# Fourier mixing and soft mixture of experts: batch 0's first transform with the tokens stationary, reordered on chip, and batch 1 in fp32r throughout

## The chip, the cores and the metric

One core of a Trainium2 chip. A core has TensorE (PE, matmuls; PEld is its weight load), VectorE (DVE), ScalarE (ACT), GpSimd (POOL) and SyncE (SP, which here only issues DMAs). The metric is the time of one execution of the whole kernel in microseconds (us), measured on the device; lower is better.

## The reference

```python
x = attn_in                                  # 8 batches, 2496 tokens, 256 wide, float32
X = np.fft.rfft(x, axis=1)                   # over the tokens
Yr = Xr @ w_r - Xi @ w_i + b_r
Yi = Xr @ w_i + Xi @ w_r + b_i
Y  = sign(Y) * max(|Y| - 0.01, 0)            # real and imaginary part apart
y  = np.fft.irfft(Y, n=2496, axis=1)         # 19968 tokens of 256 from here
logits = y @ phi                             # 32 slots, 4 for each of 8 experts
d = softmax of logits over the tokens;  c = softmax of logits over the slots
slot_in = d.T @ y
slot_out[e] = max(slot_in[e] @ w1[e], 0) @ w2[e]
out = c @ slot_out
```

## The kernel before

2496 is 39 times 64, so the transform over the tokens is done in two steps: a **first transform** of length 39 and a **second** of length 64. A batch's tokens lie in 117 partitions (3 groups of 39) by 22 columns g of 256 numbers. By the symmetry of real input 20 of the 39 frequencies are enough, each with a cosine and a sine: 3 x 40 = 120 rows.

*First transform* (`a_unit`, one unit for two of the 22 columns). The constant matrix f1a (117 x 120) is stationary and the tokens move, 512 columns at a time. The result `pa` (120 rows) is copied from PSUM to `ast` by ACT, written to DRAM (`adr`; for the first 48 rows of batch 0 a tensor `ad0`, over ACT's own DMA queue) and read back by `load_ap` as `ap`, with a frequency's 64 columns in the partitions: the transposition between the two transforms goes through DRAM. In batches 2 to 7 a unit is done in fp32r: the tokens and the matrix are split into a rounded high part and the rest (`xh`, `xl`, `f1h`, `f1l`), and three fp32r matmuls are added up. In batch 0 (11 units) and in the first four units of batch 1 it is a plain fp32 matmul (`direct`), which the machine runs as two passes.

*The main loop* has 40 steps s: 8 batches by 5 groups of 4 frequencies. In a step:
- `f2`: two second transforms `px` (c = 0, 1: the left and right half of the 256 numbers), four fp32 matmuls each with a slice of `ap` stationary. ACT copies them to `xth` and `xsm`, DVE makes the rest `xtl`, a sum `xsm`, and its split `xsh`, `xsl` (POOL makes `xsl` after step 0).
- `lin_k`, `lin_y`: the linear layer in fp32r, `pk` of 12 and `py` of 24 matmuls, with the split weights `w_r`, `nws`, `wd` of the tensor `wri`. DVE and POOL add the bias and threshold (`ut`, `rt`).
- `tp_p`, `tp_t`: the logits `pq`, and transposes `pt` of `rt`, which ACT copies to `T`.

Around these run, with time stamps of their own, the first transforms of later batches, the softmax stages of earlier ones (`c_stages`), and after TB the expert weights, the experts and the output.

The order of all this is set by hand. A generator yields a due time from PLAN, `run_until` resumes the one that is due, and every operation is kept in program order on its engine. So an engine's queue is a fixed list, and an instruction that waits holds up what is behind it on that engine. In the opening the order of SP's queue was `PLAN["seq"]`: loads of constants and x, the loads of `ap` 0, 1 and 2, the four writes of the rest of batch 0, and two held writes of batch 1. PSUM tiles come from tags: `pf` (px, pa), `pl` (pk, py) and `pt` (pq, pt) with two banks each; a new tile of a tag waits until the old one in its bank has been read.

The profile's lines: L180 is the wrapper through which DVE, ACT and POOL operations are recorded, L237 is SP's DMA, L240 ACT's DMA, L243 a matmul, L532 a transpose.

Of the kernel before, what the change touches and what calls it, by code (L numbers as in the profile page):

```python
# [50 lines left out]
def _constants():  # L51
# [92 lines left out]
    "ws": [-29, -28.9, -28.8, 2],  # L144
# [3 lines left out]
    "kw": [[-40, 9]],  # L148
    "ap1": 1.85,
# [34 lines left out]
def fourier_soft_moe_kernel(ctx: ExitStack, tc: tile.TileContext, t: dict, out: bass.AP):  # L184
# [29 lines left out]
    cnt = {}  # L214
# [7 lines left out]
    def L_(k, s, i):  # L222
# [66 lines left out]
    while len(x0) < G // GP:  # L289
        load_x0()  # L290
# [35 lines left out]
    def a_unit(b, g, u):  # L326
        first = b == 0
        i_ = g // GP
        abounds = abounds_.get(b, abounds_[2])
        tu = u if first else PLAN["a1"][i_] if b == 1 else 20 * (b - 1) - LEAD + (2 * i_ + PLAN["au"][0] if i_ < 9 else PLAN["au"][i_ - 8])  # L330
        gs = next(a for a in abounds if a[0] <= g < a[1])
        direct = first or (b == 1 and i_ < PLAN["nd"])
# [6 lines left out]
        xs = x0[i_] if first else xrs[(b, g - g % xc)][:P1, g % xc : g % xc + GP, :]
        if not direct:  # L340
            xh = wtile([P1, GP, D], F32R, "xh", f"xh{b}_{g}")
            xl = wtile([P1, GP, D], F32R, "xl", f"xl{b}_{g}")
            if b == 1:
                split(xh, xl, xs, {"A": A, "V": V}[PLAN["h1"][i_]], {"P": P, "V": V}[PLAN["l1"][i_]])
            else:
                split(xh, xl, xs, E_("ah"), E_("al"))
        yield tu
        if g == gs[0]:
            if (b, g) in PLAN["ast4"]:
                asts[(b, g)] = wtile([QA, 4, D], F32, PLAN["ast4"][(b, g)], f"ast{b}_{g}")  # L350
            else:
                asts[(b, g)] = wtile([QA, 6, D], F32, "ast", f"ast{b}_{g}")
        ast = asts[(b, gs[0])]
        po = psum(("pf", "pl", "pt")[i_ % 3] if first else "pf", f"pa{b}_{g}")
        if direct:
            mm(out=po, lhsT=f1a, rhs=xs, start=True, stop=True)
        else:
            mm(out=po, lhsT=f1h, rhs=xh, start=True, stop=False)
            mm(out=po, lhsT=f1h, rhs=xl, start=False, stop=False)
            mm(out=po, lhsT=f1l, rhs=xh, start=False, stop=True)  # L360
        yield tu + PLAN['ao']
        copy(
            (A, V)[PLAN["e1"][i_]] if b == 1 else A,
            ast[:, g - gs[0] : g - gs[0] + GP, :].rearrange("p g d -> p (g d)"),
            po,
        )
        if g + GP == gs[1]:
            if b == 1 and direct:
                held[gs[0]] = (ad[b], ast, *gs)
                return  # L370
            yield tu + 1.0
            if first:
                a_write(ad0, ast, *gs, 0, R * 4 * KG, q=aq)
                rest.append((ad[b], ast, *gs, R * 4 * KG, QA))
            else:
                a_write(ad[b], ast, *gs)

    ad0 = dr.tile([R * 4 * KG, G, D], F32, tag="ad0", name="ad0", bufs=1)
    rest, held = [], {}

    def a_write(adr, ast, g0, g1, r0=0, r1=QA, q=sp):
        q(out=adr[r0:r1, g0:g1], in_=ast[r0:r1, : g1 - g0, :])
# [9 lines left out]
    def f2(s, c, t0):  # L392
# [21 lines left out]
        sl = wtile([128, KG, 64], F32R, "xsl", f"xsl{b}_{grp}_{c}")  # L414
        A.copy(out=xh, in_=pv)
# [7 lines left out]
        (L_("sl", s, c) if s else V).tensor_tensor(out=sl, in0=sm, in1=sh.bitcast(F32), op=ALU.subtract)  # L423
        xts[(s, c)] = (xh, xl, sh, sl)
# [20 lines left out]
    def lin_k(s):  # L445
# [10 lines left out]
    def lin_y(s, e):  # L456
# [318 lines left out]

    def wsplit2(nm, src, eh, el):
# [42 lines left out]
    for tok in PLAN["seq"]:  # L819
        one(tok)  # L820
# [442 lines left out]
```

## Time and profile before

| | |
|---|---|
| timed runs | 567.23, 565.03, 566.69 us; median 566.69 |
| profiled execution, span from first to last instruction | 561.5 us; it has no other time of its own, and the median lies 5.2 us above the span |
| PE busy | 521.4 us (93%), mean granted clock 0.989 |
| DVE, ACT, POOL busy | 422.0, 298.1, 281.1 us |
| DMA | 121.44 MB, mean 216 GB/s |

The span in 40 slices of 14 us, busy share in tenths (9 is 90% or more), and the granted clock of PE:

```profile
PE   8669999999999999999999999999899979899794
PEclk9999999999999999999999999999999998999899
```

PE is below 9 tenths in the first three slices (42 us) and here and there in the last ten; between them it is full. The chain of waits for the opening, the windows of 5 us and the timeline of each engine are the views to read here; their lines stand where they are used.

### The profile page before, as it was taken

How to read it: one execution, taken by the hardware profiler on the slowest of the kernel's cores; microseconds unless marked ns; L12 is line 12 of the kernel's file. 1: busy time of each engine (PE TensorE's matmuls, PEld its weight loads, DVE VectorE, ACT ScalarE, POOL GpSimd, SP SyncE). 2: the span in 40 equal slices, each digit the busy share in tenths (PEclk: the TensorE clock that was granted, in tenths of full speed). 3: DMA queues.
4: the chain of work that ended last, by engine and by line, in shares of the span. 5: the costliest groups of instructions: out<-in, count | busy, mean ns of one | idle time of the engine just before them, and what ended most of it. 6: DMA issues, size and time to landing. Idle time of an engine off the chain costs nothing.

```text
span 561.5 us, 11780 instructions
## 1 busy us (share of the span) xinstructions
PE 521.4 (93%) x4354; PEld 442.2 (79%) x4354; DVE 422.0 (75%) x837; ACT 298.1 (53%) x650; POOL 281.1 (50%) x258
## 2 busy tenths in 40 slices
PE   8669999999999999999999999999899979899794
PEld 4458999989898889889988898987687867367573
DVE  0347897799979897989789978986795764248783
ACT  4435555666566656665665666653433333147572
POOL 0037777766766576658655866684554402000100
PEclk9999999999999999999999999999999998999899
DMA  8788464756476637664757474766634378979898
GB/s 301 249 294 292 151 207 152 210 179 170 163 216 207 189 118 208 207 180 167 204 171 199 155 201 167 222 230 178 186 131 126 113 183 276 392 240 368 325 374 351
DMA packets 93684, 121.44 MB, mean 216 GB/s; under 512 B 46786, under 2 KB 68736, under 8 KB 93628
## 3 DMA queue, kind: packets, MB, share of 16 engines
q1 hardware_dynamic: 93372, 119.63, 65.4%
q10 hardware_dynamic: 256, 1.08, 0.5%
q8 instruction: 34, 0.56, 0.4%
q14 instruction: 22, 0.18, 0.1%
HBM read 69.87 MB, written 50.82 MB: 215 GB/s over the span
## 4 chain that ended last, share of the span: by engine, by line
PE 70%; DVE 13%; DMA 10%; ACT 3%; issue 2%; SPq 1%; ACTq 0%; DVEq 0%
PE py L243 16%; PE px L243 11%; PE pq L243 9%; PE pa L243 8%; PE pk L243 7%; PE pt L532 4%; PE pr L243 3%; DMA eb<-ed 2%; PE pc L1067 2%; DMA ad<-ast 2%; PE pe L243 2%; DMA ap<-adr 2%; DVE mx L180 1%; DVE clpL L180 1%; DVE xtl L180 1%
## 5 line engine op out<-in xcount | busy, mean ns | idle before, releaser
L180 POOL TENSOR_TENSOR rt<-ut,rt 128x512 f32<-128x512 f32 x79 | 111.7, 1414 | 24.4 <-DVE rt L180 18.4
L180 POOL TENSOR_TENSOR xsl<-xsm,xsh 128x256 fp32r<-128x256 f32 x77 | 59.3, 770 | 102.4 <-DVE xsh L180 71.0
L180 POOL TENSOR_TENSOR xl<-xr,xh 117x512 fp32r<-117x512 f32 x73 | 98.5, 1350 | 22.6 <-ACT xh L180 14.7
L243 PE MATMUL px<-smov,ap 128*128 128x128 f32 x640 | 85.6, 277 | 8.0 <-DMA ap<-adr 4.5
L243 PEld LDWEIGHTS px<-smov,ap 128*128 128x128 f32 x640 | 80.3, 193 | 13.7 <-issue 8.1
L180 ACT CAST xth<-px 128x512 fp32r<-128x512 f32 x80 | 46.8, 585 | 73.0 <-PE py L243 37.6
L180 ACT COPY ast<-pa 128x512 f32<-128x512 f32 x86 | 50.3, 587 | 64.5 <-PE pa L243 61.6
L180 DVE SCALAR_TENSOR_TENSOR ut<-py,pk,k 128x256 f32<-128x256 f32 x160 | 69.5, 475 | 15.0 <-PE py L243 13.1
L180 DVE TENSOR_TENSOR xtl<-px,xth 128x512 fp32r<-128x512 f32 x80 | 54.6, 682 | 26.8 <-ACT xsm L180 22.0
L243 PE MATMUL py<-xth,nwsh 128*128 128x256 f32 x160 | 53.5, 334 | 0.0
L180 DVE TENSOR_SCALAR rt<-ut 128x512 f32<-128x512 f32 x69 | 52.2, 756 | 0.5
L243 PE MATMUL pk<-xsh,w_rh 128*128 128x256 f32 x160 | 47.9, 300 | 2.0 <-DVE xsh L180 2.0
L180 ACT COPY T<-pt 128x512 f32<-128x512 f32 x70 | 42.1, 601 | 9.0 <-PE pt L532 7.3
L532 PE MATMUL pt<-pk,rt 128*128 128x128 f32 x320 | 45.9, 273 | 0.9 <-DVE dd L180 0.6
L243 PE MATMUL pk<-xsl,w_rh 128*128 128x256 f32 x160 | 45.1, 282 | 0.0
L243 PE MATMUL pk<-xsh,w_rl 128*128 128x256 f32 x160 | 44.9, 281 | 0.0
L243 PE MATMUL py<-xtl,nwsh 128*128 128x256 f32 x160 | 44.7, 279 | 0.0
L243 PE MATMUL py<-xtl,wdh 128*128 128x256 f32 x160 | 44.7, 279 | 0.0
L243 PE MATMUL py<-xth,wdl 128*128 128x256 f32 x160 | 44.7, 279 | 0.0
L243 PE MATMUL py<-xth,nwsl 128*128 128x256 f32 x160 | 44.7, 279 | 0.0
L243 PE MATMUL py<-xth,wdh 128*128 128x256 f32 x160 | 44.7, 279 | 0.0
L243 PE MATMUL pq<-rhs,ct 128*128 128x512 f32 x156 | 43.1, 415 | 0.3 <-DVE ost L180 0.3
(186 smaller groups left out, 1241.7 us busy)
## 6 DMA issues: line engine op xcount, KB each, us to landing
ap<-adr SPq DMA_DIRECT2D x76, 256.0 KB
out<-ost SPq DMA_DIRECT2D x37, 512.0 KB
xr<-in_x SPq DMA_DIRECT2D x35, 512.0 KB
adr<-ast SPq DMA_DIRECT2D x20, 768.0 KB
w<-in_moe_w SPq DMA_DIRECT2D x25, 512.0 KB
adr<-ast SPq DMA_DIRECT2D x8, 512.0 KB
w<-in_moe_w SPq DMA_DIRECT2D x14, 256.0 KB
x<-in_x SPq DMA_DIRECT2D x11, 256.0 KB
```

The costliest lines, as they stand in the source:

```text
L180: return lambda *a, **k: self.tc.keep_in_program_order(f(*a, **k))
L243: tc.keep_in_program_order(nc.tensor.matmul(**kw))
L532: tc.keep_in_program_order(nc.tensor.transpose(out=out, in_=in_, identity=identity))
L1067: nc.tensor.transpose(out=pc[:, i * P1 : (i + 1) * P1], in_=chls[b][x][:, 2 * (r + i) : 2 * (r + i) + 2].rearrange("p g h s -> p (g h s)") ...
```

## The change

Batch 0's first transform has its operands exchanged. Now the tokens are stationary (`x0[i][:, e, h*128 : h*128+128]`, 117 x 128, where h is the half of the 256 numbers) and the matrix moves, reordered once into `f1x`. The result `q` has the 256 numbers' half in the partitions and the frequencies in the columns. ACT copies the first group's frequencies of `q` to `at0[h]`, DVE those of the other four groups to `atr[h]`, in such an order that 128 consecutive columns hold one frequency's cosine and sine at 64 columns; then four PE transposes (`ap0(s, h)`) and one copy (ACT for h = 0, DVE for h = 1) make half of `ap` s. With 5 groups, 2 halves and 4 frequencies that is 40 transposes. Batch 0 neither writes to nor reads from DRAM between its transforms, and ACT issues no DMA there. The groups 1 to 4 are transposed when the main loop needs them (`ap_t`, times in `PLAN["t0"]`).

All eleven units of batch 1 are done in fp32r, and within the main loop; their copies are all ACT's and their writes four, as in later batches. The nine extra dummy matmuls (`keep_warm`) go. The setup of the weights (`setup`) is interleaved with the new matmuls, with two operations moved from DVE to POOL. SP loads `wri` ahead of the last five tiles of x, and `PLAN["seq"]` is gone. In step 0 the order of the split after `px` is another, and `pk` and `py` take the halves alternately. The scratch for DMA descriptors is made smaller.

```diff
-    while len(x0) < G // GP:
+    f1x = wtile([P1, 2, NGRP, KG * R], F32, "mx", "f1x")
+    V.tensor_copy(out=f1x, in_=f1a[:, :Q1].rearrange("p (a c x) -> p c a x", c=2, x=KG * R))
+    f1x = f1x.rearrange("p c a (k r) -> p c (a k) r", r=R)
+    while len(x0) < 6:
         load_x0()
...
-        if direct:
-            mm(out=po, lhsT=f1a, rhs=xs, start=True, stop=True)
-        else:
-            mm(out=po, lhsT=f1h, rhs=xh, start=True, stop=False)
...
+        mm(out=po, lhsT=f1h, rhs=xh, start=True, stop=False)
+        mm(out=po, lhsT=f1h, rhs=xl, start=False, stop=False)
+        mm(out=po, lhsT=f1l, rhs=xh, start=False, stop=True)
...
+    def q_mm(i, h):
+        qd, k = divmod(i, 2)
+        if k == 0:
+            qps[(qd, h)] = psum(("pf", "pl", "pt")[(2 * qd + h) % 3], f"q{qd}_{h}")
+        v = qps[(qd, h)][:, : 4 * Q1].rearrange("p (r k g c) -> p g c k r", r=R, g=4, c=2)
+        for e in range(GP):
+            mm(
+                out=v[:, GP * k + e],
+                lhsT=x0[i][:, e, h * 128 : h * 128 + 128],
+                rhs=f1x,
+                start=True,
+                stop=True,
+                skip_group_check=True,
+            )
+        if k == 0 and i + 1 < G // GP:
+            return
+        n = 2 * GP * (k + 1)
+        v = qps[(qd, h)][:, : 4 * Q1].rearrange("p (r k x) -> p r k x", r=R, x=8)
+        for dst, src, eng in ((at0[h], v[:, :, :KG, :n], A), (atr[h], v[:, :, KG:, :n], V)):
+            copy(eng, dst.rearrange("p (k r x) -> p r k x", r=R, x=2 * G)[:, :, :, 8 * qd : 8 * qd + n], src)
+
+    def ap0(s, h):
+        if h == 0:
+            aps[s] = wtile([128, KG, D], F32, "ap", f"ap0_{s}")
+        w = 2 * KG * NP
+        src = atr[h][:, (s - 1) * w : s * w] if s else at0[h]
+        v = src.rearrange("p (k n) -> p k n", k=KG)
+        pt = psum("pt", f"pa0_{s}_{h}")
+        for j in range(KG):
+            tr(pt[:, j * 128 : j * 128 + 128], v[:, j, : 2 * N2], ident)
+        copy((A, V)[h], aps[s][:, :, h * 128 : h * 128 + 128], pt.rearrange("p (j x) -> p j x", x=128))
...
+    def head():
...
+        for i in range(6):
+            for h in range(2):
+                q_mm(i, h)
+        for i in range(6, G // GP):
+            q_mm(i, 0)
+            if i % 2 == 0 and i < 10:
+                setup(i // 2 - 3)
+            elif i == 9:
+                setup(2)
+        for i in range(6, 8):
+            q_mm(i, 1)
+        yield t_[1]
+        ap0(0, 0)
+        yield t_[2]
+        for i in range(8, G // GP):
+            q_mm(i, 1)
+        yield t_[3]
+        ap0(0, 1)
+
+    def ap_t(s):
+        for h in range(2):
+            yield PLAN["t0"][s - 1] + 0.2 * h
+            ap0(s, h)
...
+        if s == 0:
+            A.copy(out=sm, in_=pv[:, 0])
+            A.copy(out=xh, in_=pv)
+            V.tensor_tensor(out=sm, in0=pv[:, 1], in1=sm, op=ALU.add)
+            split(sh, sl, sm, V, V)
+            V.tensor_tensor(out=xl, in0=pv, in1=xh.bitcast(F32), op=ALU.subtract)
+            return
...
+    sp(out=wri, in_=t["w"])
+    while len(x0) < G // GP:
+        load_x0()
...
-    for t_, n_ in PLAN["kw"]:
-        step_to(keep_warm(t_, n_))
...
+        elif s_:
+            step_to(ap_t(s_))
...
-    nc = _bacc.Bacc("TRN2", target_bir_lowering=False, num_devices=1)
+    nc = _bacc.Bacc("TRN2", target_bir_lowering=False, num_devices=1, dynamic_dma_scratch_size=1024)
```

The instructions in their order on an engine follow; a name is tile, batch, group or column, and number. First PE at the end of the first transform. Before:

```order
L243 MATMUL pa0_20_174<-x0_20_103,f1a_81 128x512
L243 MATMUL pa1_0_180<-xr1_0_130,f1a_81 128x512
L243 MATMUL pa1_2_183<-xr1_0_130,f1a_81 128x512
L243 MATMUL pa1_4_187<-xr1_4_134,f1a_81 128x512
L243 MATMUL pa1_6_190<-xr1_4_134,f1a_81 128x512
L243 MATMUL wps532_218<-warm_72 128x512 x9
L243 MATMUL px0_0_0_242<-smov0_109,ap0_0_194 128x128 x4
L243 MATMUL px0_0_1_247<-smov0_109,ap0_0_194 128x128 x4
L243 MATMUL pk0_0_274<-xsh0_0_0_255,w_rh_228 128x256
```

The same place with the change:

```order
L233 MATMUL q3_1_222<-f1x_83,x0_14_124 128x2x20x3 x2
L595 MATMUL pa0_0_0_230<-pk0_104,at0_0_142 128x128 x4
L233 MATMUL q4_1_236<-f1x_83,x0_16_126 128x2x20x3 x2
L233 MATMUL q4_1_236<-f1x_83,x0_18_128 128x2x20x3 x2
L233 MATMUL q5_1_243<-f1x_83,x0_20_130 128x2x20x3 x2
L233 MATMUL px0_0_0_248<-smov0_101,ap0_0_229 128x128 x4
L595 MATMUL pa0_0_1_253<-pk0_104,at0_1_144 128x128 x4
L595 MATMUL pa0_1_0_260<-pk0_104,atr0_143 128x128 x4
L233 MATMUL px0_0_1_266<-smov0_101,ap0_0_229 128x128 x4
L595 MATMUL pa0_1_1_271<-pk0_104,atr1_145 128x128 x4
L233 MATMUL pk0_0_308<-xsh0_0_0_280,w_rh_191 128x256
```

The four units of batch 1 and the dummies are gone from there, and groups 0 and 1 of `ap` are transposed around the two px. DVE at the start of step 0, before:

```order
L180 SCALAR_TENSOR_TENSOR nwsl_235<-wsum_193,nwsh_234 128x512
L180 TENSOR_TENSOR xtl0_0_0_253<-px0_0_0_242,xth0_0_0_252 128x512
L180 TENSOR_TENSOR xsm0_0_0_254<-px0_0_0_242,xsm0_0_0_254 128x256
L180 CAST xsh0_0_0_255<-xsm0_0_0_254 128x256
L180 TENSOR_TENSOR xsl0_0_0_256<-xsm0_0_0_254,xsh0_0_0_255 128x256
```

With the change:

```order
L174 COPY atr1_145<-q5_1_243 128x3x16x4
L174 COPY ap0_0_229<-pa0_0_1_253 128x4x128
L174 COPY ap0_1_259<-pa0_1_1_271 128x4x128
L174 TENSOR_TENSOR xsm0_0_0_279<-px0_0_0_248,xsm0_0_0_279 128x256
L174 CAST xsh0_0_0_280<-xsm0_0_0_279 128x256
L174 TENSOR_TENSOR xsl0_0_0_281<-xsm0_0_0_279,xsh0_0_0_280 128x256
L174 TENSOR_TENSOR xtl0_0_0_278<-px0_0_0_248,xth0_0_0_277 128x512
```

The copies of `ap` 0 and 1 (right halves) now stand ahead of the split of the first px, and in the split `xtl` comes last. Last, PE in step 1, around the logits of step 0 (`pq0_0`), with the change:

```order
L595 MATMUL pa0_3_0_545<-pk0_104,atr0_143 128x128 x4
L233 MATMUL pq0_0_559<-rt0_0_0_356,pk0_104 32x128 x4
L233 MATMUL pq0_0_559<-rt0_0_1_441,pk0_104 32x128 x4
L595 MATMUL pa0_3_1_568<-pk0_104,atr1_145 128x128 x4
L233 MATMUL pa1_14_574<-xh1_14_490,f1h_97 128x512
L233 MATMUL pa1_14_574<-xl1_14_491,f1h_97 128x512
L233 MATMUL pa1_14_574<-xh1_14_490,f1l_98 128x512
```

Before, the same place held the two rows of `pq0_0` and the three of `pa1_14` without the two rows of transposes (L595).

More of the change, by code (lines that the diff above doesn't have):

```diff
@@ L326, in a_unit @@
     def a_unit(b, g, u):
[L327 removed]
         i_ = g // GP
[L329 to L330 removed]
+        tu = PLAN["a1"][i_] if b == 1 else 20 * (b - 1) - LEAD + (2 * i_ + PLAN["au"][0] if i_ < 9 else PLAN["au"][i_ - 8])
         gs = next(a for a in abounds if a[0] <= g < a[1])
[L332 removed]
@@ L333, in a_unit @@
-        if not first and g % xc == 0:
+        if g % xc == 0:
             yield PLAN["x1"].get((b, g), tu - 6)
             load_x(xorder.index((b, g)))
-        yield tu - (2.7 if first else PLAN["ap1"] if b == 1 else 1.95)
+        yield tu - (PLAN["ap1"] if b == 1 else 1.95)
         if g == 0:
             ad[b] = dr.tile([QA + 1, G, D], F32, tag="adr", name=f"adr{b}", bufs=3)
[L339 to L344, printed above, removed]
-            else:
-                split(xh, xl, xs, E_("ah"), E_("al"))
+        xs = xrs[(b, g - g % xc)][:P1, g % xc : g % xc + GP, :]
@@ L347, in a_unit @@
+        xh = wtile([P1, GP, D], F32R, "xh", f"xh{b}_{g}")
+        xl = wtile([P1, GP, D], F32R, "xl", f"xl{b}_{g}")
+        if b == 1:
+            split(xh, xl, xs, A, {"V": V, "P": P}[PLAN["l1"][i_]])
+        else:
+            split(xh, xl, xs, E_("ah"), E_("al"))
         yield tu
         if g == gs[0]:
[L349 to L352, printed above, removed]
+            asts[(b, g)] = wtile([QA, 6, D], F32, "ast", f"ast{b}_{g}")
@@ L367, in a_unit @@
[L367 to L382, printed above, removed]
+        po = psum("pf", f"pa{b}_{g}")
@@ new lines, in fourier_soft_moe_kernel, with wpair, setup @@
+    wr_, wi_ = wri[:, 0:2, :], wri[:, 2:4, :]
+    def wpair(nm):
+        wts[nm] = tuple(wmp.tile([128, 2, D], F32R, tag=nm + z, name=nm + z) for z in "hl")
+        return wts[nm]
+    def setup(i):
+        if i == 0:
+            split(*wpair("w_r"), wr_, V, V)
+        elif i == 1:
+            wsum = wtile([128, 2, D], F32, "k1", "wsum")
+            P.tensor_tensor(out=wsum, in0=wr_, in1=wi_, op=ALU.add)
+            h, l = wpair("nws")
+            A.mul(out=h, in_=wsum, mul=-1.0)
+            V.scalar_tensor_tensor(
+                out=l, in0=wsum, scalar=-1.0, in1=h.bitcast(F32), op0=ALU.mult, op1=ALU.subtract
+            )
+        else:
+            P.tensor_tensor(out=wi_, in0=wi_, in1=wr_, op=ALU.subtract)
+            split(*wpair("wd"), wi_, A, P)
@@ L384, in load_ap @@
+    def ap_t(s):
+        for h in range(2):
+            yield PLAN["t0"][s - 1] + 0.2 * h
+            ap0(s, h)
     def load_ap(b, grp):
         ap = wtile([128, KG, D], F32, "ap", f"ap{b}_{grp}")
-        src = (ad0 if b == 0 and grp < 2 else ad[b]).rearrange("(k r) g d -> k (r g) d", r=R)
+        src = ad[b].rearrange("(k r) g d -> k (r g) d", r=R)
         src = src[grp * 2 * KG : (grp + 1) * 2 * KG, :N2]
@@ L450, in lin_k @@
         for c in range(2):
+            if s == 0 and c:
+                yield t0 + 1.01
             lin_s(pk, c, xts[(s, c)])
-        yield t0 + PLAN['ko']
+        yield t0 + (PLAN['ko'] if s else 1.02)
         kss[s] = wtile([128, 2, 256], F32, "k1", f"k1{b}_{g}")
@@ L888, in ap_load @@
         aps[s] = load_ap(*steps[s])
-    def keep_warm(t, n):
-        yield t
-        ps = psum("ps", f"wps{next(seq)}")
-        for _ in range(n):
-            mm(out=ps, lhsT=warm[:, 0:128], rhs=warm, start=True, stop=True)
-    for t_, n_ in PLAN["kw"]:
-        step_to(keep_warm(t_, n_))
     for s_ in range(ns):
-        if s_ not in aps:
+        if s_ >= NGRP:
             step_to(ap_load(s_))
+        elif s_:
+            step_to(ap_t(s_))
         for c in range(2):
```

105 lines of the change are left out of this document (30 added, 75 removed).

## The prediction

> **What bounds the kernel now.** I read the page's totals first, then the windows over the whole span, then the chain of waits for the first 65 us, because the change touches only the opening.
>
> ```profile
> span 561.5 us, 11780 instructions
> PE 521.4 (93%) x4354; PEld 442.2 (79%) x4354; DVE 422.0 (75%) x837; ACT 298.1 (53%) x650; POOL 281.1 (50%) x258
> ```
>
> ```profile
> 0.00:5.00 5.00, 3.55 (x7) 2.32 (x8) 1.00 (x3) 1.28 (x1) 0.42 (x6) 1.00 0.55 159
> 5.00:10.00 5.00, 5.00 (x12) 2.11 (x11) 0.00 (x0) 2.63 (x5) 0.00 (x0) 1.00 1.02 377
> ...
> 20.00:25.00 5.00, 3.33 (x22) 2.69 (x21) 0.69 (x1) 1.76 (x4) 1.29 (x1) 1.00 0.77 228
> 25.00:30.00 5.00, 3.04 (x20) 2.32 (x20) 3.40 (x8) 1.46 (x5) 0.00 (x0) 1.00 0.96 327
> ...
> 35.00:40.00 5.00, 1.28 (x11) 1.07 (x10) 2.48 (x7) 0.59 (x1) 2.80 (x3) 1.00 0.68 201
> 40.00:45.00 5.00, 5.00 (x29) 4.71 (x28) 0.00 (x0) 2.44 (x5) 1.27 (x1) 0.66 1.00 350
> ...
> 60.00:100.00 40.00, 40.00 (x368) 36.91 (x358) 33.92 (x69) 23.20 (x52) 29.80 (x27) 1.00 0.49 159
> ```
>
> TensorE (PE) is the bound: in a windows row the number after the comma is its busy time, 40.00 of 40 us in the last row. Between 35 and 40 us it works 1.28 of 5 us, and in the next row its granted clock (third from the end) is 0.66; the last number is what the DMA moved, in GB/s. The chain says what it waited for.
>
> ```profile
> 8.60 5.60 DMA ad<-ast
> ...
> 23.53 2.04 PE px L243 x16
> ...
> 31.32 1.80 PE px L243 x16
> ...
> 35.53 4.01 DMA ap<-adr
> 39.54 0.14 issue
> 39.68 1.72 PE px L243 x8
> 41.39 1.28 PE pa L243 x3
> 42.67 1.82 PE pk L243 x12
> ...
> 60.34 0.90 PE py L243 x6
> ```
>
> Batch 0 goes to DRAM (`ad<-ast`) and comes back (`ap<-adr`); the first second transform (`px`) starts at 23.53 and the third group's at 39.68, after a wait for its load. From the py at 60.34 on (the second half of py of step 2) both programs issue the same PE instructions in the same order, to the end. PE is full there, and what follows is triggered by buffers that come free, not by a clock of its own. So I ask one thing: **when does the changed kernel reach that py?** The span moves by that difference.
>
> **The change part by part.** Three stretches: A to the first px; B to the end of py of step 0 (31.32 before, where the next px starts); C to 60.34.
>
> ```profile
> 5.37 0.34 PEld L243 LDWEIGHTS pa<-x,f1a 117*128 117x128 f32 x1 [0.52 <-DMA x<-in_x]
> ```
>
> ```profile
> 52.17 0.44 PE pt L532 x4
> 52.61 0.89 PE px L243 x8
> 53.50 1.42 PE pk L243 x12
> ...
> 55.36 0.70 PE pa L243 x3
> ...
> 59.77 0.57 PE pq L243 x16
> ```
>
> ```profile
> L180 DVE TENSOR_TENSOR dd<-pd,pk 128x320 f32<-128x320 f32 x16 | 7.7, 482 | 2.0 <-PE pd L243 2.0
> ```
>
> A. The first matmul on x starts at 5.37, when its tile lands; the new one waits for the same tile. There are 44 new matmuls, each fp32 and therefore two passes: 88 passes of 120 moving columns on a stationary of 128. No row shows this form (its output is scattered over a PSUM bank). The nearest is px, also fp32 with 128 columns: 0.89/8 = 0.111 to 2.04/16 = 0.128 a pass; I take 0.118, the middle: 10.4 us, to 15.8. One group of four transposes stands among them (the pt row: 0.44), so the first px starts at 16.2, **7.3 earlier** than 23.53. What hides the loads: f1a, 11 tiles and the weights moved ahead of the last five are 3.5 MB. Before, 2.7 MB had moved by 10.0 (159 GB/s, then 377, five us each), so at 377 the last tile lands near 12.1; PE reaches it after 64 passes, at 12.9. If that 0.8 of cover is gone, the delay is paid in full. The twelve small copies on each of ACT and VectorE (DVE), 96 and up to 384 elements long, cost about 0.5 each by the 128x320 row, 6 us on each engine within 10: hidden beside the passes. The nine dummy matmuls (wps) that go stood in idle time, and the two sums of the weights that move from DVE to GpSimd (POOL) run while POOL has nothing else to do (0.00 busy from 5 to 10): nothing. The smaller descriptor scratch only frees memory, as far as I can read; nothing.
>
> ```profile
> 25.59 0.69 DVE L180 TENSOR_TENSOR xtl<-px,xth 128x512 fp32r<-128x512 f32 x1 [3.91 <-PE px L243]
> 26.19 0.41 DVE L180 TENSOR_TENSOR xsm<-px,xsm 128x256 f32<-128x256 f32 x1
> 26.64 0.29 DVE L180 CAST xsh<-xsm 128x256 fp32r<-128x256 f32 x1
> 26.97 0.43 DVE L180 TENSOR_TENSOR xsl<-xsm,xsh 128x256 fp32r<-128x256 f32 x1
> 27.31 0.68 DVE L180 TENSOR_TENSOR xtl<-px,xth 128x512 fp32r<-128x512 f32 x1
> ```
>
> ```profile
> L180 DVE COPY ast<-pa 128x512 f32<-128x512 f32 x2 | 1.4, 684 | 0.2 <-PE pa L243 0.2
> ```
>
> B. DVE now copies the right halves of ap 0 and ap 1 out of PSUM before it splits the first px, and queued behind the second copy is the whole split of step 0, for which pk and py wait. Path: px 0.89, transposes 0.44, copy 0.68 and some 0.1 of drain, the second px 0.89, transposes 0.44, copy 0.8, then twice the split's round of 1.72 (25.59 to 27.31), and the last py passes, 0.5: 16.2 + 8.2 = 24.4. I take 24.5 against 31.32: **6.8 earlier**. B is 0.5 longer than before: the copies are paid here.
>
> C. PE's work in C before, by the rows above: 7 fp32r pa of three passes (0.70) 4.9; 6 px (0.89) 5.3; 78 pk and py passes (1.42/12) 9.2; two pq 1.1; two pt and a small transpose 1.0; together 21.5. It took 29.0, so 7.5 went to waits: 3.7 for the ap load, about 1.8 for the slow clock behind it (1.72 against 0.89, 1.28 against 0.70, 1.82 against 1.42), and 2.0 of others. The change adds the four pa of batch 1 that stood in the idle opening (now three fp32r passes each, 2.8) and six of the ten transpose groups (2.6): 27.0. The ap wait and its slow clock go, with all of batch 0's DRAM traffic, and on SP's queue the loads of x no longer stand behind it. **What is late next** is ACT.
>
> ```profile
> L180 ACT COPY ast<-pa 128x512 f32<-128x512 f32 x29 | 16.8, 586 | 21.5 <-PE pa L243 18.7 <-issue 1.3 <-DMA ad<-ast 0.9
> L180 ACT CAST xth<-px 128x512 fp32r<-128x512 f32 x16 | 9.4, 586 | 17.2 <-PE px L243 9.7 <-PE py L243 7.5
> L180 ACT CAST xh<-xr 117x512 fp32r<-117x512 f32 x13 | 8.1, 629 | 5.4 <-DMA xr<-in_x 5.4
> L180 ACT COPY xsm<-px 128x256 f32<-128x256 f32 x16 | 6.1, 380 | 0.0
> ```
>
> ```profile
> L180 DVE CAST xsh<-xsm 128x256 fp32r<-128x256 f32 x80 | 34.6, 432 | 2.7
> ```
>
> ACT gets 11 casts of x, 11 copies of pa and three of ap in C, some 39 operations of 0.4 to 0.6 in 29 us. I walked through C by hand, in the order of the engines' rows, with these durations: px of step 1, right half, needs pa 2's bank, whose copy stands behind the copy of pa 0, a cast of x and both reads of the left px: 1.0 of idle. Three smaller waits behind ACT come to 0.6 (pa 6, the second transposes of group 3, pa 16); each of these waits for one ACT copy that I find queued behind another operation of 0.4 to 0.6. xsh on DVE is longer over the whole run (432 ns) than in the quiet opening (0.29), and some three of them lie on the path: 0.4. Together 2.0, and I count 2.2 for what such a walk misses. The bounds of this unknown are 0, PE never kept waiting, and the 7.5 of before; I stay near 0 because what caused most of the 7.5 is gone. C ends at 24.5 + 27.0 + 2.2 = 53.7 against 60.34.
>
> Batch 1's write and load do not get in the way: its last copy (pa 20) is near 52 and its first px stands about 11 us of PE work behind the common py, near 64; the load took 4.0 (`ap<-adr`) and a write at most 5.6 (`ad<-ast`), 9.6 of 12.
>
> **Sum:** 60.3 - 53.7 = 6.6; span 561.5 - 6.6 = 554.9. The timed runs have a median of 566.69, 5.2 above this execution's span, and I keep that: **560.1 us**.
>
> **The rivals.** (1) *ACT replaces the DMA.* In C ACT serves pa, px, ap and T in one fixed order; each late copy holds a PSUM bank. For it: DVE is at 34 of 40 us in the full rows and ACT's load in C is above its 23 of 40. Against it: PE and ACT have little queued behind loads now. If C loses as much as before (7.5), the time is 560.1 + 5.5 = 565.6, no change that can be measured. (2) *The clock falls again.* From 15.8 to 24.5 PE works in short bursts with transposes between them. If the clock halves once, the price is the 1.8 above: 561.9. For it: it fell after the 3.71 us gap; against it: in the same stretch of before, gaps of 1.67 and 1.44 left it at 1.00 (rows 20 to 30 above).
>
> ```profile
> 23.53 2.02 PE L243 MATMUL px<-smov,ap 128*128 128x128 f32 x16 [1.67 <-DMA pk<-in_pk]
> ...
> 26.99 0.39 PE L243 MATMUL pk<-xsh,w_rh 128*128 128x256 f32 x1 [1.44 <-DVE xsh L180]
> ...
> 39.68 1.72 PE L243 MATMUL px<-smov,ap 128*128 128x128 f32 x8 [3.71 <-DMA ap<-adr]
> ```
>
> The Trainium skill's page "TensorE: Matmul & The Clock Gate" (Part 1) says that PE drops to half its clock after an idle window of about 3.4 us, with which these rows agree; its Part 4 says that transposes do not count as activity. By that rule the stretch from 15.8 to 24.5, with 16 transposes in it, is nearer to idle than it looks, which is rival 2 and its 561.9.
>
> (3) *The new matmul is dear.* Its output goes to PSUM in steps, 160 elements apart at the innermost. If a pass costs more than px's, all of A grows: the upper neighbour is a pass of pa with 512 columns.
>
> ```profile
> 4.38 10.44 PE L243 MATMUL pa<-x,f1a 117*128 117x512 f32 x22
> ```
>
> From 5.37 to 14.82 that is 0.43 a pass; 88 of them cost 27.5 more than I count, 587.6, **slower**. It decides from 0.118 + 6.6/88 = 0.193 a pass on. Against it: every other matmul here goes by its moving columns. (4) *No waits in C at all:* 558.1.
>
> That the change doesn't do what it says I leave out: the rows show the transposes and batch 1's three passes.
>
> **How the numbers follow.** Forecast 0.60; rival 1 0.12; rival 2 0.12; rival 3 0.05; rival 4 0.11. A measurement of this kernel can tell about 0.5% (2.8 us) from no change: forecast, rivals 2 and 4 are faster (0.83), rival 1 is the same (0.12), rival 3 is slower (0.05). The forecast's own spread is about 2 us either way, from the pass at 0.111 or 0.128 (0.6 to 0.9) and the waits in C; the range 557.4 to 564.4 holds it with rivals 2 and 4 and part of the way to rival 1, and leaves out less than 0.2.
>
> **What would show it.** Right: first px near 16, the end of the first py near 24.5, the common py near 53.7, clock 1.00 from 35 to 45 us, no wait for `ap<-adr` before 60 us, and the same length from there to the end. Wrong: q passes above 0.19; idle of PE before px or pa that ends with an ACT copy, beyond 2 us in all; or the lead at the common py lost again later.

## The result, and the profile after

The changed kernel takes 561.1 us (median of 8 runs, 559.51 to 562.47), the kernel before 565.88 in 8 runs beside it (562.54 to 568.14). The ratio is 0.9912 (95% interval 0.9883 to 0.9942): 4.8 us less, somewhere from 3.3 to 6.6. The forecast was 560.1. Its single steps come out less well than its sum. The page's totals for the changed kernel:

```profile
span 560.1 us, 11969 instructions
PE 523.6 (93%) x4455; PEld 452.0 (81%) x4455; DVE 433.6 (77%) x854; ACT 299.9 (54%) x662; POOL 286.2 (51%) x261
```

TensorE is busy for 2.2 us more than before (521.4) and DVE for 11.6 more, in which the new copies and splits are. The windows of 5 us over the opening, with the columns of the prediction's rows (PE's busy time behind the comma, its granted clock third from the end):

```profile
5.00:10.00 5.00, 4.69 (x22) 4.72 (x23) 1.11 (x2) 0.48 (x2) 0.00 (x0) 1.00 1.00 363
10.00:15.00 5.00, 5.00 (x46) 5.00 (x46) 2.97 (x6) 1.75 (x7) 2.53 (x2) 1.00 1.04 382
...
35.00:40.00 5.00, 4.91 (x36) 4.51 (x35) 4.93 (x8) 3.75 (x9) 3.74 (x3) 1.00 0.37 110
40.00:45.00 5.00, 4.80 (x46) 3.89 (x44) 2.64 (x7) 2.49 (x5) 4.50 (x4) 1.00 0.73 253
```

The hole at 35 to 45 us is gone (4.91 and 4.80 busy; before 1.28, and 5.00 at clock 0.66). But the first two rows hold something odd: PE is busy in both, and gets through 22 matmuls in the first and 46 in the second. Lines here are L174 for DVE, ACT and POOL, L233 for a matmul, L595 for a transpose. The new matmuls `q` by tile, their count and their shortest, median and longest record in ns, first from 6.5 to 9 us, then from 11 to 16 us:

```profile
L233 PE MATMUL q<-f1x,x x13: 421/421/421, 6.3 to 8.8; 117*128 117x120 f32 x13
L233 PE MATMUL q<-f1x,x x47: 275/275/275, 10.8 to 15.9; 117*128 117x120 f32 x47
```

421 ns is what the px records showed in before's row of granted clock 0.66, 275 what they show elsewhere. So TensorE runs at about half speed here until about 10 us, although the column says 1.00. The packed trace of after, from which the views are made, holds no entry of the granted clock before 10.04 us, the moment of the turn, and the column counts a stretch without an entry as full: its 1.00 there is no measurement. The chain of waits (start, duration, what) gives the milestones:

```profile
5.31 10.97 PE q L233 x76
16.28 0.44 PE pa L595 x4
16.72 1.33 PE q L233 x12
18.05 0.90 PE px L233 x8
...
24.95 1.39 DVE xsl L174
...
26.38 0.74 PE pk L233 x4
27.11 0.71 PE py L233 x6
...
30.31 0.62 ACT ast L174
...
30.97 1.16 PE px L233 x8
...
57.05 0.67 PE pa L595 x4
57.74 0.69 DVE ap L174
```

First px at 18.05 (forecast 16.2), the end of step 0's first py at 27.8 (24.5), the common py near 57.7 (53.7; before 60.34). In this execution the lead at the common py is 2.6 us, not 6.6, and the spans differ by 1.4. Three questions follow: why A and B are long, where the lead goes behind the common py, and how medians 4.8 apart come from spans 1.4 apart.

### The profile page after: what moved, and what is told of

It is laid out like the page before. It is cut to its first block, busy times and chain, and to the rows that moved or that the text cites. A ratio compares the mean times of both kernels' runs of the same rounds, so it can differ in the third digit from the quotient of the medians.

```text
span 560.1 us, 11969 instructions
## 1 busy us (share of the span) xinstructions
PE 523.6 (93%) x4455; PEld 452.0 (81%) x4455; DVE 433.6 (77%) x854; ACT 299.9 (54%) x662; POOL 286.2 (51%) x261
## 4 chain that ended last, share of the span: by engine, by line
PE 68%; DVE 15%; DMA 8%; ACT 4%; issue 3%; SPq 1%; ACTq 0%; DVEq 0%
PE py L233 14%; PE px L233 10%; PE pq L233 9%; PE pa L233 7%; PE pk L233 6%; PE pt L595 4%; PE pr L233 3%; DMA eb<-ed 3%; PE q L233 2%; PE pc L1084 2%; DVE xtl L174 2%; DMA ed<-ea 2%; DVE mx L174 1%; DMA gp<-gd 1%; PE pe L233 1%
## 5 line engine op out<-in xcount | busy, mean ns | idle before, releaser
L174 POOL TENSOR_TENSOR rt<-ut,rt 128x512 f32<-128x512 f32 x79 | 112.5, 1424 | 21.5 <-DVE rt L174 17.4
L174 POOL TENSOR_TENSOR xl<-xr,xh 117x512 fp32r<-117x512 f32 x74 | 100.4, 1357 | 25.5 <-ACT xh L174 17.7
L174 POOL TENSOR_TENSOR xsl<-xsm,xsh 128x256 fp32r<-128x256 f32 x77 | 59.1, 767 | 105.6 <-DVE xsh L174 73.5
L233 PE MATMUL px<-smov,ap 128*128 128x128 f32 x640 | 85.6, 277 | 2.8 <-DVE xsm L174 1.6
L233 PEld LDWEIGHTS px<-smov,ap 128*128 128x128 f32 x640 | 80.1, 192 | 9.1 <-PE pa L233 2.6
L174 ACT CAST xth<-px 128x512 fp32r<-128x512 f32 x80 | 46.9, 587 | 64.1 <-PE py L233 34.4
L174 DVE SCALAR_TENSOR_TENSOR ut<-py,pk,k 128x256 f32<-128x256 f32 x160 | 69.5, 475 | 12.7 <-PE py L233 10.8
L174 ACT COPY ast<-pa 128x512 f32<-128x512 f32 x77 | 45.4, 589 | 57.4 <-PE pa L233 57.3
L174 DVE TENSOR_TENSOR xtl<-px,xth 128x512 fp32r<-128x512 f32 x80 | 54.6, 683 | 20.6 <-ACT xsm L174 20.5
L233 PE MATMUL py<-xth,nwsh 128*128 128x256 f32 x160 | 53.3, 333 | 0.0
L174 DVE TENSOR_SCALAR rt<-ut 128x512 f32<-128x512 f32 x69 | 52.4, 759 | 0.5
L233 PE MATMUL pk<-xsh,w_rh 128*128 128x256 f32 x160 | 48.3, 302 | 1.4 <-DVE xsh L174 1.4
L174 ACT COPY T<-pt 128x512 f32<-128x512 f32 x70 | 42.0, 601 | 9.0 <-PE pt L595 7.3
L595 PE MATMUL pt<-pk,rt 128*128 128x128 f32 x320 | 45.8, 273 | 0.9 <-DVE dd L174 0.6
L233 PE MATMUL pk<-xsl,w_rh 128*128 128x256 f32 x160 | 45.5, 284 | 0.9 <-DVE xsl L174 0.9
L233 PE MATMUL pk<-xsh,w_rl 128*128 128x256 f32 x160 | 45.2, 283 | 0.0
L233 PE MATMUL py<-xtl,nwsh 128*128 128x256 f32 x160 | 44.7, 279 | 0.0
L233 PE MATMUL py<-xtl,wdh 128*128 128x256 f32 x160 | 44.7, 279 | 0.0
L233 PE MATMUL py<-xth,nwsl 128*128 128x256 f32 x160 | 44.7, 279 | 0.0
L233 PE MATMUL py<-xth,wdl 128*128 128x256 f32 x160 | 44.7, 279 | 0.0
L233 PE MATMUL py<-xth,wdh 128*128 128x256 f32 x160 | 44.7, 279 | 0.0
L233 PE MATMUL pq<-rhs,ct 128*128 128x512 f32 x156 | 42.7, 413 | 0.0
```

What stands on the lines that cost most here:

```text
L174: return lambda *a, **k: self.tc.keep_in_program_order(f(*a, **k))
L233: tc.keep_in_program_order(nc.tensor.matmul(**kw))
L595: tc.keep_in_program_order(nc.tensor.transpose(out=out, in_=in_, identity=identity))
```

## The experiments

The table has all traces, before's too. A is the start of the first px, B from there to the first pa or px behind step 0's first py, C from there to the common py, D from the common py to the first px of batch 1, each as a difference of starts in PE's timeline (which shows a start some 0.15 earlier than the chain). "Rest" is the span behind D. The second column is the median q record from 6.5 to 9 us. The timed runs were taken in groups, each on one chip with its own runs of before, whose medians were 565.88 (after), 565.55 (warm8, direct4, t0late), 564.79 (combo) and 566.22 (three, after_again), so across groups the ratios to before are what can be compared.

| kernel | q, ns | A | B | C | D | rest | median of timed runs |
|---|---|---|---|---|---|---|---|
| before | | 23.53 | 7.63 | 29.11 | 11.28 | 490.0 | 565.88 |
| before_again | | 24.43 | 7.57 | 29.98 | 11.27 | 489.0 | (563.98, one run) |
| before_3 | | 23.16 | 7.58 | 29.76 | 11.27 | 489.5 | (563.12, one run) |
| before_4 | | 23.19 | 7.63 | 31.07 | 11.28 | 492.8 | (567.8, one run) |
| after | 421 | 17.89 | 9.77 | 29.80 | 12.10 | 490.5 | 561.1 |
| after_again | 275 | 16.50 | 9.78 | 29.75 | 12.09 | 488.7 | 561.55 |
| warm1 | 421 | 16.80 | 9.78 | 29.74 | 12.09 | 489.8 | (560.4, one run) |
| warm8 | 275 | 16.30 | 9.79 | 29.76 | 12.10 | 490.7 | 560.27 |
| direct4 | 275 | 17.06 | 8.78 | 29.83 | 12.09 | 491.5 | 561.32 |
| l1v | 421 | 18.14 | 8.79 | 29.76 | 12.08 | 490.3 | (561.15, one run) |
| t0late | 275 | 17.16 | 6.98 | 30.48 | 12.09 | 491.1 | 559.42 |
| sclate | 275 | 16.24 | 9.77 | 29.76 | 11.64 | 488.9 | (558.45, one run) |
| combo | 275 | 18.67 | 6.98 | 30.48 | 12.08 | 490.8 | 560.14 |
| three | 275 | 16.75 | 6.98 | 30.46 | 11.62 | 490.9 | 558.84 |

In the changed kernel B, C and D repeat to 0.1 us as long as their order of work is the same. An edit that shortens B or D is seen there at once, where the timed runs of one kernel scatter by 2 to 8 us. A is the part that scatters in the opening, and the rest scatters as in before.

**A: dummies at the start.** Eight in warm8; in warm1 the 8 is a 1.

```diff
-    for _ in range(6):
+    for _ in range(8):
         mm(out=wps, lhsT=warm[:, 0:128], rhs=warm, start=True, stop=True)
```

> The kernel after with eight dummy matmuls at the start in place of six, so that TensorE is not idle for the 0.93 us before the first tile of x. Theory (TensorE runs at half clock until 9.7 us because of that gap; a q record is 421 ns there, 275 behind it): the records go to 275 ns by about 7 us, the first px stands at 16.0 to 17.0 instead of 18.05, and the run is 1 to 2 us shorter than after (559 to 560). Rival (the x tiles arrive at that pace, one of 256 KB per 1.2 us or so): the q passes keep a pitch of 0.22 us until 10 us, the first px stays at 18, the time stays at 561.

> The kernel after with one dummy matmul at the start in place of six. Theory (TensorE's clock rises only after some 3.4 us of nearly unbroken work, at a point of its own that differs from run to run): the q records are 421 ns from their start at about 5 us until at least 8.5 us, in every execution, so the first px comes at 17.5 to 19. Rival (the dummies do nothing, the clock of the opening is chance alone): in this look the records are at 275 ns by 6 to 7 us, as in three of the four traces of this opening so far.

By tile from 6.5 to 9 us, first warm8, then warm1:

```profile
L233 PE MATMUL q<-f1x,x x23: 274/275/421, 6.1 to 8.9; 117*128 117x120 f32 x23
```

```profile
L233 PE MATMUL q<-f1x,x x15: 275/421/421, 6.2 to 9.0; 117*128 117x120 f32 x15
```

warm8 has its last record of 421 ns at 6.51 us, turns to 275 by 6.8, and its first px comes at 16.30, 1.6 before that of after: the pace to 10 us was the clock's, not the arrival of x. warm1 has its last record of 421 ns from 8.33 to 8.75 us, so that it turns where I had set it (8.5 or later), but its first px at 16.80 misses the 17.5 to 19; one trace cannot settle what one dummy does.

Among the traces with six dummies two (after, l1v) are slow until about 10 us and four (after_again, direct4, t0late, sclate) are fast by 6 us or earlier; three traces with eight (warm8, three, combo) turn by about 7.7 at the latest. With six dummies it is the arrival of the first x tile that tells the two groups apart: `q` starts at 5.31 and 5.34 in the slow ones, behind 0.93 and 0.96 us of idle time, and at 4.18 to 4.67 in the fast ones, behind at most 0.29. PE's timelines of after and of after_again:

```profile
5.31 0.97 PE L233 MATMUL q<-f1x,x 117*128 117x120 f32 x3 [0.93 <-DMA x<-in_x]
```

```profile
4.39 1.78 PE L233 MATMUL q<-f1x,x 117*128 117x120 f32 x8
```

That fits a clock which rises after some microseconds without a gap, at a moment of its own, and which misses its moment where the x tile comes late and leaves a gap. So the clock's late rise is not chance alone, as I wrote in what I expected of after_again: in these six traces it comes with a late tile. It isn't proved that eight dummies always help: warm8's median, 560.27 (559.51 to 564.05), cannot be told from after's.

The Trainium skill's page "TensorE: Matmul & The Clock Gate" (Part 1) says that the window in which activity is judged, of about 3.4 us, runs freely, so that the point of the rise varies from run to run. The turns of the three traces with eight dummies and no gap, near 5.3 us (three), 6.8 (warm8) and 7.7 (combo), agree with it.

**B: what DVE does before and beside step 0's split.** t0late moves the transposes and copies of the second group's ap behind the split:

```diff
-    "t0": [-1.9, 2.45, 6.4, 10.4],
+    "t0": [-1.3, 2.45, 6.4, 10.4],
```

l1v puts two splits of batch 1 on DVE in place of POOL:

```diff
-    "l1": 'VPPVPPVPPPP',
+    "l1": 'VVVVPPVPPPP',
```

direct4 takes the first four units of batch 1 back to plain fp32, without their xh and xl:

```diff
+        direct = b == 1 and i_ < 4
...
+        if direct:
+            mm(out=po, lhsT=f1a, rhs=xs, start=True, stop=True)
```

> The kernel after with the transposes and the copy of the second group's ap behind the split of step 0 (one number in the plan). Theory (DVE's copy of ap 1 at 21.80 holds up the split of the first px, which is ready from 21.2, and with it pk and py of step 0): the first xsm on DVE at about 21.3 instead of 22.41, the end of step 0's first py about 1 us earlier than 27.8, the run 0.5 to 1 us shorter than after. Rival (the split waits for ACT's casts anyway, and the transposes moved behind px now stand in front of pk): the end of py stays at 27.8 within 0.3 and the time at 561.

> The kernel after with the first four units of batch 1 as one fp32 matmul each again (two passes of 512 columns, no casts and splits of x), as they were before: that part of the change alone undone. Theory (POOL's splits xl of batch 1 beside step 0's split make DVE's xsl 1.38 us instead of 0.43, and those units' casts load ACT): xsl back at 0.43, the end of step 0's first py 0.9 earlier than 27.8, in C four units at 0.87 instead of 0.70 give back 0.7 and fewer waits for ACT and DVE gain some 0.5: the run 0 to 1.5 us shorter than after (560.3). Rival (the xsl was long for another reason, and three fp32r passes are cheaper): the run is 0.7 us longer than after, 561.8.

> The kernel after with the splits xl of batch 1's second and third unit on DVE in place of POOL (two letters of the plan; TensorE's order is the same). Theory (POOL's subtraction, running beside it, stretches DVE's xsl from 0.43 to 1.38): the second xsl of step 0 is 0.43, and the stretch from the first px to the end of step 0's first py is 8.8 long, as with direct4, not 9.8. Rival (direct4 gained by having fewer casts on ACT): xsl stays near 1.4 or the stretch at 9.8.

DVE's and POOL's timelines of after, from the copy of ap 1 on:

```profile
21.80 0.69 DVE L174 COPY ap<-pa 128x512 f32<-128x512 f32 x1 [1.69 <-PE pa L595]
22.41 0.41 DVE L174 TENSOR_TENSOR xsm<-px,xsm 128x256 f32<-128x256 f32 x1
22.86 0.29 DVE L174 CAST xsh<-xsm 128x256 fp32r<-128x256 f32 x1
23.19 0.42 DVE L174 TENSOR_TENSOR xsl<-xsm,xsh 128x256 fp32r<-128x256 f32 x1
23.53 0.68 DVE L174 TENSOR_TENSOR xtl<-px,xth 128x512 fp32r<-128x512 f32 x1
24.13 0.41 DVE L174 TENSOR_TENSOR xsm<-px,xsm 128x256 f32<-128x256 f32 x1
24.58 0.33 DVE L174 CAST xsh<-xsm 128x256 fp32r<-128x256 f32 x1
24.95 1.38 DVE L174 TENSOR_TENSOR xsl<-xsm,xsh 128x256 fp32r<-128x256 f32 x1
```

```profile
23.34 2.70 POOL L174 TENSOR_TENSOR xl<-xr,xh 117x512 fp32r<-117x512 f32 x2 [6.03 <-ACT xh L174]
```

DVE's timeline of l1v, the same second xsl:

```profile
25.16 0.42 DVE L174 TENSOR_TENSOR xsl<-xsm,xsh 128x256 fp32r<-128x256 f32 x1
```

And DVE's of t0late, the first split:

```profile
18.69 0.69 DVE L174 COPY ap<-pa 128x512 f32<-128x512 f32 x1 [0.69 <-PE pa L595]
19.30 0.41 DVE L174 TENSOR_TENSOR xsm<-px,xsm 128x256 f32<-128x256 f32 x1
```

In after DVE sits idle for 1.69 until ap 1's transposes are there, with the first px already done behind that copy. t0late takes the px and its split first: B is 6.98 in place of 9.77, far more than the 1 us I expected. The second px gains nothing (it starts 2.28 behind the first in both). What I had not seen is that ACT's copy of ap 1 moves too, which in after stood ahead of ACT's reads of the first px, and DVE's split needs these. ACT's timelines of after and of t0late, where the px start at 17.89 and 17.16:

```profile
19.86 0.59 ACT L174 COPY ap<-pa 128x512 f32<-128x512 f32 x1 [1.57 <-PE pa L595]
20.34 0.38 ACT L174 COPY xsm<-px 128x256 f32<-128x256 f32 x1
```

```profile
18.25 0.37 ACT L174 COPY xsm<-px 128x256 f32<-128x256 f32 x1 [0.70 <-PE px L233]
```

So DVE's first xsm comes 2.14 behind the px in place of 4.52, and DVE's last xsl ends at 22.74, before POOL starts at 23.10. C gives back 0.7 (30.48): unit 0's xl now stands behind the moved copy, and its pa waits 0.47 for it. t0late takes 559.42 (557.57 to 561.52), ratio to before 0.9881 (0.9848 to 0.9914), which overlaps after's interval. l1v separates the rest: with the same TensorE order and the two subtractions on DVE, xsl is 0.42 again and B 8.79. So **1.0 us of B was POOL working beside DVE**, and the order cost 1.8 more, on DVE and ACT together: t0late moves the copies of both and doesn't tell them apart.

direct4 has the same B as l1v, 8.78, and pays nothing for it in C (29.83). Its time is 561.32 (557.91 to 562.41), after's own; neither theory's number is told from the other by it. To the resolution of these runs batch 1 in fp32r neither gains nor costs, so what the change brings lies in its other parts. That it is the reordering on chip is argued from the waits that are gone; no run takes it, the order of the loads or the dropped dummies back by itself.

**D: the lead that is lost behind the common py.**

```diff
-    "sc": [4.7, 8.7, 12.7, 16.7],
+    "sc": [4.7, 8.7, 15.0, 16.7],
```

> The kernel after with the split of f1 (f1h and f1l, 1.11 and 1.28 us on DVE) moved from 61.3 us to behind the next group's rt, where DVE sat idle for 1.03. Theory (behind the common py TensorE is ahead of DVE, and gives back 0.7 us of the lead because DVE's row of work with f1h and f1l in it sets the next px): from the common py to the first px of batch 1 it takes 11.4 to 11.7 us in place of 12.1 in the traces of after, warm8, t0late and direct4. Rival (DVE is full there whatever its order): 12.1 again, or more because the next split waits.

DVE's timeline of after, up to the px at 65.14, which waits for DVE's xsm, and PE's timeline in the second fence:

```profile
57.74 0.69 DVE L174 COPY ap<-pa 128x512 f32<-128x512 f32 x1 [3.10 <-PE pa L595]
58.35 0.42 DVE L174 TENSOR_SCALAR rt<-ut 128x512 f32<-128x512 f32 x1
...
59.28 0.41 DVE L174 TENSOR_TENSOR xsm<-px,xsm 128x256 f32<-128x256 f32 x1
...
61.31 1.11 DVE L174 CAST f1h<-pk 117x120 fp32r<-117x120 f32 x1
62.45 1.28 DVE L174 TENSOR_TENSOR f1l<-pk,f1h 117x120 fp32r<-117x120 f32 x1
63.65 0.41 DVE L174 TENSOR_SCALAR rt<-ut 128x512 f32<-128x512 f32 x1
63.99 0.68 DVE L174 TENSOR_TENSOR xtl<-px,xth 128x512 fp32r<-128x512 f32 x1
64.59 0.41 DVE L174 TENSOR_TENSOR xsm<-px,xsm 128x256 f32<-128x256 f32 x1
```

```profile
59.80 1.16 PE L233 MATMUL px<-smov,ap 128*128 128x128 f32 x8
...
65.14 1.13 PE L233 MATMUL px<-smov,ap 128*128 128x128 f32 x8 [0.21 <-DVE xsm L174]
```

DVE's row runs without a pause from the copy of the last ap at 57.74 to that px. TensorE is ahead of it and gives back 0.8 us (D is 12.1 against 11.28). With f1's split later D is 11.64, within the expected 11.4 to 11.7: a bit more than half of the loss was its place in DVE's queue. Of the rest, 0.27 falls at the px at 59.80, which comes 2.34 behind the common py in after and in sclate and 2.07 in before. It starts 0.1 behind the end of DVE's xsm of 59.28, and ahead of that in DVE's queue stands the copy of the last ap, for which DVE sat idle for 3.10. That this copy is the cause, by its place as in B, is not shown: no run moves it. The row of sclate's f1l shows why it cost so little there: it fell into a pause of POOL's and took 0.28, not 1.28.

```profile
65.61 0.28 DVE L174 TENSOR_TENSOR f1l<-pk,f1h 117x120 fp32r<-117x120 f32 x1
```

**All together.** combo is warm8 and t0late with the weights' load (wri) behind the ninth x tile in place of the sixth; three is warm8, t0late and sclate.

```diff
-    sp(out=wri, in_=t["w"])
     while len(x0) < G // GP:
         load_x0()
+        if len(x0) == 9:
+            sp(out=wri, in_=t["w"])
```

> The kernel after with three edits together: eight dummies (warm8), the copies of ap 1 behind step 0's split (t0late), and the weights' load moved from behind the sixth to behind the ninth tile of x. Theory (with the clock up, TensorE waits 0.6 to 0.7 for the seventh tile of x, which stands behind the weights; the gains add up): no wait for x after the first tile, first px at 15.5 to 16.3, first py of step 0 ends 7.0 later, common py at 53 to 53.8, the run 0.5 to 1.5 us shorter than t0late (558 to 559). Rival (the weights come too late for their splits, or q then waits for the copies out of PSUM): first px at 17 again or pk waiting for w_r, the time at 559.4 or above.

> The kernel after with the three edits that showed a gain in their stretch: eight dummies, ap 1's copies behind step 0's split, f1's split later; the weights' load where after has it. Theory (each edit keeps the gain that its stretch showed: on average some 0.8 from the clock, 2.5 in the stretch from the first px to the end of step 0's first py, 0.5 behind the common py): first px at 16.2 to 17.2, that stretch 7.0, common py at 52.8 to 54.0, first px of batch 1 at 64.5 to 65.7, the run 3 to 4 us shorter than after measured beside it (557 to 558 if after is at 561). Rival (the gains are eaten again, as in combo): common py above 54.5 or a time within 1.5 of after.

> The kernel after, unchanged, beside the other on the same chip. Theory (its first trace had a late clock in the opening, 421 ns records until 9.7 us, and a drop near 410 us): 560.5 to 561.5 again; the records of q go to 275 ns either by about 6 us or only at 8.5 to 10.5 us, by chance, the first px at 16.2 to 17.2 or at 18, the stretch from it to the end of step 0's first py at 9.8 in either case. Rival (the opening of after is slow as a rule): above 561.5, records at 421 ns to 8.5 us or later.

combo's theory fell in A: first px at 18.67. DVE's timeline of combo:

```profile
12.60 1.31 DVE L174 CAST w_rh<-wri 128x512 fp32r<-128x512 f32 x1
13.95 1.64 DVE L174 TENSOR_TENSOR w_rl<-wri,w_rh 128x512 fp32r<-128x512 f32 x1
15.51 0.55 DVE L174 COPY atr<-q 128x384 f32<-128x384 f32 x1
15.98 1.63 DVE L174 SCALAR_TENSOR_TENSOR nwsl<-wsum,nwsh 128x512 fp32r<-128x512 f32 x1
17.53 2.00 DVE L174 COPY atr<-q 128x384 f32<-128x384 f32 x5
```

In after these three took 0.42, 0.69 and 0.68, from 13.95 on. The weights come later, so POOL's work on them (12.35 to 17.06) now runs beside DVE's splits, which take two to three times as long, and the copies of q queue up behind them. By PE's timeline TensorE then waits 0.57 for ACT's at and 0.74 for DVE's atr, as the rival had it. The wait for the seventh x tile that I wanted to remove was only 0.6. The time is 560.14 (557.85 to 562.58), the rival's too.

three keeps the load where it was. A (16.75), B (6.98) and C's end (common py at 54.19) lie within what was expected or 0.2 off, the first px of batch 1 at 65.81 just behind the 64.5 to 65.7. It takes 558.84 us (557.86 to 559.94); after beside it 561.55 (558.91 to 562.82) and before 566.22. The ratio to before is 0.9855 (0.9818 to 0.9891), after's there 0.9905 (0.987 to 0.994). By medians three is 2.7 us shorter than after, less than the 3 to 4 expected, and it has the lowest median of the kernels timed in several rounds. after_again stays with the first measurement of after (0.05 above the 560.5 to 561.5 expected), with a fast opening this time (A 16.50) and the same B, C and D.

**before again.** Three more traces of the unchanged kernel, to see what its first one was.

> The kernel before, unchanged, for a second trace of its opening. Theory (the first trace of before was a fortunate execution): its clock came up early there, with pa passes of 592 ns from 6 us on; here they stay at 871 ns or more until 8 to 11 us, the first px starts 1 to 3 us later than 23.5, and the common py (second half of py of step 2) comes at 62 to 64 instead of 60.34. Rival (the opening is always the same, the times differ in the tail): the common py stands at 60.3 within 0.5, and what differs lies behind 380 us.

> The kernel before, unchanged, a third trace. What is open: by the traces the changed kernel reaches batch 1's first px 3.6 us earlier on average (72.4 in the two traces of before, 68.8 in after's), but the medians differ by 4.7. Theory (before's opening, which goes through DRAM behind loads, varies more and both traces of it were short ones): the first px of batch 1 at 73 to 75.5. Rival (the rest lies behind it): 71.5 to 73, and the span from there to the end longer than the 490.0 and 489.0 of the two traces.

> The kernel before, unchanged, a fourth trace, with the same question as the third: batch 1's first px at 73 to 75.5 if it is the opening that varies, at 71.5 to 73 if it is what comes behind.

The first px of batch 1 comes at 71.55, 73.25, 71.77 and 73.17. The theory of a lucky first trace is half right at most: it is the shortest of the four in the opening, but before_again's first px of all (A) comes only 0.9 later and its common py at 61.98, both just short of what was expected, before_3 is hardly longer, against expectation, and before_4's 566.0 of span comes mostly from a rest of 492.8. The rest is 490.3 on average in before's four traces and in the ten others alike. It goes with how often the clock falls in it. By the packed traces the granted clock is halved for 3.41 us at a time; not counting the last 6 us of the span, that happens behind D once in after_again, sclate, before_again and warm1 (rest 488.7 to 489.8), twice in eight traces (489.5 to 491.5), and three times in t0late and before_4 (491.1 and 492.8). Whether the clock or the waits ahead of its falls cost the time is not shown.

## Why the prediction was right, and where its steps were not

- **The question itself** (which wait goes, and that the lead at the common py decides) held. No wait for `ap<-adr` is left before 60 us, no clock drop at 40, and the rest behind D is as long as before on average.
- **A** was given as 16.2. Four traces of the same opening with the clock up gave 16.24 to 17.16, the two with it late 17.89 and 18.14; the mean of the six is 17.17. The step that failed is "I take 0.118, the middle": the pass is 0.111 to 0.12 at full speed, but about twice as long until the clock has risen. I took the 1.00 in the clock column of 0 to 10 us at its word, while before's own first dummies and pa, in the same trace, had longer records than later ones. The cover that I named for the loads (0.8) was not there: in two of the four traces with the clock up TensorE waited some 0.6 for the seventh x tile (direct4: the q at 11.23, behind 0.59; t0late 0.67).
- **B** was given as 8.3 and is 9.78. "The copies are paid here" was right. What the walk through DVE's queue left out is POOL's xl beside it: 1.0 us (l1v), by one instruction of 1.38 in place of 0.43. I had seen xsh at 432 ns on average against 0.29 in quiet, and charged it to C alone. The other 0.5 lies in pieces of 0.2 to 0.3 along the path. That path went by DVE's copies only; ACT's copy of ap 1 ahead of its reads of px, which t0late showed, isn't in it.
- **C** was given as 27.0 of work and 2.2 of waits, 29.2. It is 29.74 to 29.83: 0.6 off. Its two terms are further off than their sum, in opposite directions: in after's C (the row below, PE's busy time behind the comma) TensorE is busy for 28.50 and idle for 1.30. The wait before px for ACT's copy of pa, which the walk found at 1.0, is 0.8 in the profile, ahead of the px at 30.97.

```profile
27.66:57.46 29.80, 28.50 (x226) 25.04 (x225) 21.25 (x38) 19.36 (x41) 18.32 (x16) 1.00 0.52 171
```

- **The same length from the common py on** failed: D is 12.1 against 11.28. "PE is full there" was true of before, where TensorE was the late engine. Once it comes earlier DVE is the late one, and 0.8 of the lead goes there, which the sum had at nothing.
- **The sum.** The lead of 6.6 at the common py shrinks by 1.0 in A, 1.5 in B and 0.6 in C to 3.6 against that one trace of before, and D takes 0.8 more. Against the mean of before's four traces (first px of batch 1 at 72.4) the mean opening of the changed kernel (17.17 + 9.78 + 29.76 + 12.10 = 68.8) is 3.6 us earlier; the timed medians differ by 4.8 and 4.7. The four profiled executions of before had run times of about 564.6 on average (with 2.0 around the first one's span), and its medians in the four larger groups of timed runs lie between 564.8 and 566.2, so up to 1.6 us can be the choice of the profiled executions. That this is all of the difference is not shown.
- **The 5.2 us around the span** was wrong: the runs show 1.8 to 2.2 between a run's span and its time. The other 3 us were that the profiled execution was a short one. So 560.1 came from a lead that was too large, taken off a base that was too high. The same working with 2.0 around the span would have given 556.9, below the range; with the lead measured against that trace at batch 1's first px, 2.7 (71.55 less 68.8), it gives 560.8. So the two errors cancel, and it is luck that 560.1 lies within 1.0 of the 561.1 measured. What held is the direction and its reason, the wait for `ap<-adr` that goes; the size of the gain, 6.6, did not (4.8 measured).
- **The rivals.** (1) ACT in the DMA's place: C's length less the 27.0 of counted work is 2.8, and TensorE's idle time 1.30, not 7.5. (Rivals 1 and 4 were priced with 2.0 of waits where the sum has 2.2; with 2.2 they are 565.4 and 557.9.) (2) The clock falling again: not where I put it; in the stretch with the transposes the px records are 275 ns (row below). The rule cited from the Trainium skill's "TensorE: Matmul & The Clock Gate" (Part 4), that transposes do not count as activity, shows no effect there. What the clock cost, it cost at the very start, by rising late: A is 18.0 on average in the two traces where it did, 16.7 in the four others. (3) The dear matmul did not come: 12 q passes take 1.33 us, 0.111 each. (4) Nor did a C without waits.

PE's px in after_again, by tile from 16 to 31 us, across the stretch with the transposes:

```profile
L233 PE MATMUL px<-smov,ap x32: 272/275/377, 16.5 to 30.5; 128*128 128x128 f32 x32
```

## What to carry to other kernels

A span from one profile is one draw: compare stretches between fixed instructions, which here repeat to 0.1 us while the order of work is the same, and keep the scattering ends (the clock's rise at the start, the tail in which it falls again) out of a forecast's base. When an engine that set the pace comes earlier, ask at the first common instruction which engine is late there now, and take its lead, not that of the engine that was moved. Before work is put on an idle engine, look at what runs beside it: two subtractions on an idle POOL cost 1.0 us on the path.

## What the runs showed of the hardware

- TensorE's speed at the start shows in the length of its records (421 ns against 275 for one form), not in the clock column, which read 1.00 through both: in all fourteen packed traces the granted clock has no entry before its first rise (4.77 to 10.53 us).
- POOL's work slows DVE's down by form. Beside POOL's xl at 23.34, DVE's xtl and xsm, which read px from PSUM, kept 0.68 and 0.41, while xsl, with two operands in SBUF, went from 0.42 to 1.38; w_rh, a cast within SBUF, went from 0.42 to 1.31 in combo. The Trainium skill's "GPSIMD Engine Reference" (1. Specifications) says that POOL shares its SBUF interfaces with VectorE, with contention for instructions that have two SBUF inputs or use a two-port mode; these rows agree for the first kind, and no run here shows which mode the cast was in.
- The q matmuls, whose output goes to PSUM in steps, take 0.111 a pass of 120 columns; px, with 128 columns in order, takes 0.111 too.
